# Sums of tiles 0 to 3 inside down's rounds, one sum of each pair in its bank, and down in a written order

## The chip, the cores and the metric

The kernel runs on one core of a Trainium2 chip. The core has five engines with a queue of instructions each: TensorE (PE, matrix products into PSUM banks), VectorE (DVE), ScalarE (ACT), GpSimd (POOL) and SyncE (SP), whose queue here only issues DMA transfers. An engine runs its queue in order, and an instruction that waits for another engine's result holds up everything behind it. The metric is the device time of one execution in microseconds, lower is better.

## The reference

An attention block with a learned feature map is multiplied by a gate from a SwiGLU block and added to the input. S = 2048 tokens, D = 1024, 32 heads of 32, F = 3584, all in fp32.

```python
xn = _layernorm(x)
q, k, v = split(xn @ wqkv)                      # 32 heads
phi_q = concat(softmax(q @ w_phi), softmax(-(q @ w_phi)))   # phi_k alike
kv, z = phi_k^T v, sum over s of phi_k
o = (phi_q @ kv) / (phi_q . z + 1e-6)
s = o @ wo
out = (silu(xn @ w1) * (xn @ w3)) @ w2
return x + s * silu(out)
```

## The kernel before

All large products run on PE as 128x128x512 matmuls in three passes over split operands (a high and a low part, written by `split`: ACT casts the high part, DVE subtracts it to get the low one). Each 2x2 block product is done with seven products instead of eight (`ORDER`: A11 x B11, A12 x B21, S2 x T2, S1 x T1, S3 x T3, S4 x B22, A22 x T4), whose partial sums share three kinds of PSUM bank: `a` for A12, `b` for A11, S2, S3 and A22 one after another, `c` for S1 and S4. A product can go into a bank only when the result of the one before has been read from it.

The stages are: gate and up products with w1 and w3; keys, values and queries; *down* (the product with w2); and the *output stage* (attention, product with wo, gate, store).

**The query stage** (`query_features`) does not divide the softmax of the queries. It writes exp(q - max) and exp(min - q) of every tile of 128 tokens to DRAM (`e_d`) and the ratio of the two sums to `rho_d`. The division by `phi_q . z` is left for later: for a tile t the *sums* are formed in steps. `z_products` multiplies e by z on POOL (two halves of 128x1024), `z_sums` reduces by head on DVE (two halves), `weigh` multiplies by rho on POOL, `add_pairs` adds pairs of partition groups with one small matmul on PE into a tile called `us`, `invert` takes the reciprocal on DVE, `factors` multiplies by rho again on POOL. Then `scale` multiplies e by the factors and `turn_e` transposes it, both in two halves on DVE.

**Down** runs in 56 rounds: round r = 8 kb + i, for 7 slices kb of w2's rows and 8 pairs i of token tiles. A round has seven products of six matmuls, in the order of `TURN`: S1, A11, S3, A12, S4, S2, A22, numbered m = 0 to 6. A11, A12 and S2 belong to the round's own pair (`old` is the pair before, whose S1, S3, S4 and A22 run one round late). `first_parts` and `second_parts` make the split operands from h, loaded by `load_h` into `hr`: `sm` (L953), then halves named `af` and `as` (L93), and `s` (L965, L966). The results are summed over kb in `acc`, two slabs of 128x1024 for a pair: DVE adds a bank to it (L1171), and in the first slice ACT copies it (L1165). The first block C11 gets two products: ACT copies A11's bank into `u` (L1168), POOL adds `u` (L1169), and DVE adds bank a. Weights of w2 come through `load_b` into a ring of 24 buffers, which later also takes wo's tiles (`load_wo`, `wos`) and small tables.

In the last slice (rounds 48 to 55) `gate` applies silu on ACT to the pair that was finished two rounds before and stores it to `g_d` from SP's queue, and the dictionary `pieces` puts the sums of tiles 0, 1 and 2 at given products: for tile 0 the products at (1,5), the sums at (2,5) and (2,6), add_pairs at (3,0), scale at (3,5) and (3,6), turn_e at (4,5) and (4,6); for tile 1 from (5,5) to (7,1); for tile 2 products and sums from (7,5) on. The first number is i, the second m.

**What sets the order.** `in_order` lists the engines whose instructions run in the order in which they are written; for others a scheduler sets the order at build time. In down it is SP's alone up to round 5, no engine's from round 6 to 47, and all engines' from round 48 on, output stage included. Waits between engines are put in by the framework in any case.

**The output stage** goes over 16 tiles t. For each, `out_half(t, 0)` and `out_half(t, 1)` multiply the attention of the tile (`oT`) by wo, 24 matmuls each; between them come `scale` and `turn_e` of tile t+1, the sums' steps for tiles t+2 and t+3, `gated` (DVE multiplies by the gate `g`, POOL adds x), and `attend(t+1, c)`, 64 small matmuls into `po`, from which ACT and DVE make the next `oT`.

Of the kernel before, what the change touches and what calls it, by code (L numbers as in the profile page):

```python
# [17 lines left out]
P = 128  # L18
# [11 lines left out]
def tile_kernel(ctx: ExitStack, tc: tile.TileContext, x, wkT, wqT, wv, wphi, wo, w1, w3, w2, out):  # L30
# [151 lines left out]
    small.tile([P, PAD], F, name="pad", bufs=1)  # L182
# [740 lines left out]
    def ring(name):  # L923
        nonlocal ring_at
        k = ring_at % 24
        ring_at += 1
        if k < 8:
            return bpa.tile([P, 2, 512], R, name=name, tag=f"ra{k}")
        if k < 20:
            return bpb.tile([P, 2, 512], R, name=name, tag=f"rb{k}")  # L930
        return late_rw[(k - 20) // 2][:, k % 2]
# [51 lines left out]
    ready = []  # L983
# [12 lines left out]
    for c in range(3):  # L996
# [5 lines left out]
        for pos, i in enumerate(order):  # L1002
            nxt, end = {}, pos + 1 == len(pairs)

            def steps():
                halves = []
                for j in range(7):
# [10 lines left out]
                    if end and j in NEXT[c]:  # L1018
                        wbn.update(fetch(3 + c, NEXT[c][j]))
                    if end and last and j in (1, 4):  # L1020
                        ready.append(a_first(0, 0) if j == 1 else a_second(*ready[0]))
# [23 lines left out]
    wos, xrs, ezs, us = {}, [], [], {}  # L1045
# [14 lines left out]

    def load_kvz():
        e0 = [slot_f("e0") for _ in range(2)]
        zb, kvs, w, own = (slot_f(name) for name in ("zb", "kvs", "rho", "own"))
        for a in range(2):
            for s in range(2):
                sl = slice(64 * a + 32 * s, 64 * a + 32 * s + 32)
                nc.sync.dma_start(zb[sl], z_d[s:s + 1].rearrange("s c g n -> s (c g n)").to_broadcast([32, D]))
                nc.sync.dma_start(kvs[sl].rearrange("p (j n) -> p j n", j=4),
                                  kv_d[:, :, s].rearrange("j f c g d -> f j (c g d)"))
            nc.gpsimd.memset(w[64 * a:64 * a + 32], 1.0)  # L1070
            nc.sync.dma_start(w[64 * a + 32:64 * a + 64].rearrange("p (t g n) -> p t g n", t=NT, g=2),
                              rho_d[a].rearrange("g i t n -> i t g n"))
        pairs_of = own[:, :P]
        nc.gpsimd.memset(pairs_of, 0.0)
        for n in range(4):
            sl = slice(32 * n, 32 * n + 32)
            for s in range(2):
                m = 32 * (n // 2 * 2 + s)
                nc.gpsimd.tensor_copy(pairs_of[sl, m:m + 32], ident[sl, sl])
        ezs.extend(slot_f("ez") for _ in range(2))  # L1080
        return (e0, zb, kvs.rearrange("p (j c g d) -> p j c g d", j=4, c=2, g=4),
                w.rearrange("p (t g c h) -> p t c g h", t=NT, g=2, c=2), own)
# [7 lines left out]
    def load_e(t):  # L1090
        if t >= NT:
            return
        for a in range(2):
            for s in range(2):
                sl = slice(64 * a + 32 * s, 64 * a + 32 * s + 32)
                src = e_d[t][64 * a:64 * a + 64, :, s * 512:s * 512 + 512].rearrange("(g i) c n -> i c g n", g=2)
                if t:
                    m = (12, 14, 8, 10)[t % 4]
                    nc.sync.dma_start(slabs[sl, m:m + 2].rearrange("i c (g n) -> i c g n", g=2), src)
                else:  # L1100
                    for c in range(2):
                        nc.sync.dma_start(e0[c][sl].rearrange("i (g n) -> i g n", g=2), src[:, c])

    def col(m):
        return own[:, P + 64 * m:P + 64 * m + 64]

    def wide(v):
        return v.rearrange("p (c g h) -> p c g h", c=2, g=2)

    def z_products(t):  # L1110
        if t < NT:
            for c in range(2):
                e = e_slab(t, c).rearrange("p (g n) -> p g n", g=2)
                nc.gpsimd.tensor_mul(ezs[c].rearrange("p (g n) -> p g n", g=2), e,  # L1114
                                     zb[:, c * 512:c * 512 + 512].unsqueeze(1).to_broadcast([P, 2, 512]))

    def z_sums(t, c):
        if t < NT:
            nc.vector.tensor_reduce(col(1 + t % 2)[:, 32 * c:32 * c + 32], ezs[c].rearrange("p (n f) -> p n f", f=DH),  # L1119
                                    axis=AX.X, op=OP.add)  # L1120

    def weigh(t):
        if t < NT:
            nc.gpsimd.tensor_mul(wide(col(0)), wide(col(1 + t % 2)), w_all[:, t])

    def add_pairs(t, tag):
        if t < NT:
            us[t] = ps.tile([P, 512], F, name="us", tag=tag, bufs=1)[:, :64]
            nc.tensor.matmul(us[t], own[:, :P], col(0), start=True, stop=True)

    def invert(t):
        if t < NT:
            nc.vector.reciprocal(col(3 + t % 2), us.pop(t))

    def factors(t):
        if t < NT:
            nc.gpsimd.tensor_mul(wide(col(0)), wide(col(3 + t % 2)), w_all[:, t])

    def scale(t, c):
        if t < NT:  # L1140
            e3 = e_slab(t, c).rearrange("p (n f) -> p n f", f=DH)
            nc.vector.tensor_mul(e3, e3, col(0)[:, 32 * c:32 * c + 32].unsqueeze(2).to_broadcast([P, H, DH]))

    def turn_e(t, c):
        if t < NT:
            nc.vector.transpose(et_slab(t, c), e_slab(t, c))  # L1146

    def product(kb, i, bank, r, ao, b, an, bn):
        c11, c12, c21, c22 = acc_of(i)
        first = b not in bank  # L1150
        if first:

            tag = "kv" if b == "c" and r > 1 and r % 3 == 2 else f"bk{b}"
            bank[b] = ps.tile([P, 512], F, name=f"bank{b}", tag=tag, bufs=1 if tag == "kv" else BANKS[b])
# [9 lines left out]
        if kb == 0 and an in ("A11", "S2", "S1", "A22"):  # L1164
            nc.scalar.copy(c, pb)  # L1165
        elif an == "A11":
            u = work.tile([P, 512], F, name="u", tag="h1", bufs=2)
            nc.scalar.copy(u, pb)  # L1168
            nc.gpsimd.tensor_add(c, c, u)  # L1169
        else:  # L1170
            nc.vector.tensor_add(c, pb, c)  # L1171
# [5 lines left out]
    pieces = {  # L1177
        (1, 5): [lambda: z_products(0)],
        (2, 5): [lambda: z_sums(0, 0)],
        (2, 6): [lambda: z_sums(0, 1), lambda: weigh(0)],  # L1180
        (3, 0): [lambda: add_pairs(0, "kv")],
        (3, 1): [lambda: invert(0), lambda: factors(0)],
        (3, 5): [lambda: scale(0, 0)],
        (3, 6): [lambda: scale(0, 1)],
        (4, 5): [lambda: turn_e(0, 0)],
        (4, 6): [lambda: turn_e(0, 1)],
        (5, 5): [lambda: z_products(1)],
        (6, 5): [lambda: z_sums(1, 0)],
        (6, 6): [lambda: z_sums(1, 1), lambda: weigh(1)],
        (7, 0): [lambda: add_pairs(1, "kv")],  # L1190
        (7, 1): [lambda: invert(1), lambda: factors(1)],
        (7, 5): [lambda: z_products(2)],
        (8, 4): [lambda: z_sums(2, 0)],
        (8, 6): [lambda: z_sums(2, 1)],
    }
    old, banks, first, second = None, {}, ready[0], None
    ahead = {}
# [63 lines left out]
    for k in range(14, 16):  # L1261
        load_wo(k)
# [125 lines left out]
```

## Time and profile before

| | us |
|---|---|
| median of 3 runs (2399.95 to 2402.06) | 2401.25 |
| the profiled execution's own time | 2401.13 |
| its span, first to last instruction | 2399.3 |
| PE busy | 2360.1 |
| down's first product begins | 1629.89 |
| A11 of round 50, of round 55 begins | 2103.01, 2162.99 |
| first `po` of the output stage | 2176.80 |

The profile is of one execution. Times in it are microseconds from the span's start. A row of a timeline has the start, the duration (of a merged row, from the first start to the last end), the engine, the line of the kernel, the operation with its output and inputs, the shape and the number of instructions; a bracket gives the idle time before it and the instruction that ended that. PE's ends are modelled, and neighbouring products overlap by a sixth of a microsecond in the rows, so PE's pace is read from start to start. "PEclk" or "granted clock" is the share of PE's clock that was granted.

### The profile page before, as it was taken

The numbers are of one execution on the slowest core, as the hardware profiler recorded it, in microseconds if no ns is written. First come the engines' busy times: TensorE is split into PE (matmuls) and PEld (weight loads), VectorE is DVE, ScalarE is ACT, GpSimd is POOL, SyncE is SP. The second block draws the span as 40 slices with busy tenths as digits, with TensorE's granted clock in tenths as the row PEclk, the third lists the DMA queues.
The fourth block names the chain that finished last, engine by engine and source line by source line (L and its number), as shares of the span: only waits on it lengthen the run. The fifth ranks groups of instructions, "written<-read, shape, count | busy, mean of one in ns | idle before, by whom it ended". The sixth has DMA issues, their size and how long they took to land. (4 is left out here: it accounts for less than half of the span.)

```text
span 2399.3 us, 37196 instructions
## 1 busy us (share of the span) xinstructions
PE 2360.1 (98%) x14354; PEld 1938.1 (81%) x14354; DVE 1776.9 (74%) x2779; ACT 855.1 (36%) x1501; POOL 253.2 (11%) x249
## 2 busy tenths in 40 slices
PE   7999999999999999999999999999999999998999
PEld 6788888888888888888788888887888888876887
DVE  8877787765788888864566666777687887796775
ACT  6445455443454555442222212334322222241000
POOL 1000000000000000000000001331011111223662
PEclk9999999999999999999999999999999999999999
DMA  5446799976988888865978878976543344448773
GB/s 213 149 157 207 238 349 336 327 254 201 288 298 295 294 271 304 278 233 189 372 265 303 288 234 336 374 263 238 184 176 109 129 176 176 136 151 299 220 206 120
DMA packets 290066, 578.00 MB, mean 241 GB/s; under 512 B 24529, under 2 KB 140385, under 8 KB 287201
## 3 DMA queue, kind: packets, MB, share of 16 engines
q1 hardware_dynamic: 285280, 558.85, 68.3%
q10 hardware_dynamic: 4608, 16.78, 1.7%
q8 instruction: 113, 1.85, 0.3%
q14 instruction: 65, 0.52, 0.1%
HBM read 370.54 MB, written 205.00 MB: 240 GB/s over the span
## 5 line engine op out<-in xcount | busy, mean ns | idle before, releaser
L93 DVE TENSOR_TENSOR bo<-rw,bo 128x512 fp32r<-128x512 f32 x336 | 230.8, 689 | 158.7 <-ACT bo L92 158.5
L92 ACT CAST bo<-rw 128x512 fp32r<-128x512 f32 x336 | 206.4, 617 | 12.9 <-DMA w_d2B<-w2o 3.3
L1159 PE MATMUL bankb<-bo,as 128*128 128x512 f32 x816 | 201.8, 390 | 3.3 <-DVE acc L1171 2.8
L1159 PEld LDWEIGHTS bankb<-bo,as 128*128 128x128 f32 x816 | 153.0, 188 | 36.4 <-DVE acc L1171 3.3
L598 PE MATMUL bankb<-op0S,bo 128*128 128x512 f32 x672 | 164.6, 394 | 1.9 <-ACT op0S L92 1.2
L598 PE MATMUL bankc<-op0S,bo 128*128 128x512 f32 x672 | 162.2, 391 | 0.0
L598 PE MATMUL bankb<-op1S,bo 128*128 128x512 f32 x672 | 161.4, 389 | 0.1
L598 PE MATMUL bankc<-op1S,bo 128*128 128x512 f32 x672 | 161.2, 389 | 0.0
L598 PE MATMUL bankb<-op0A,bo 128*128 128x512 f32 x672 | 159.6, 391 | 0.8 <-DVE bo L93 0.5
L598 PE MATMUL bankb<-op1A,bo 128*128 128x512 f32 x672 | 157.6, 390 | 0.0
L771 POOL MEMSET ev<- 128x32 f32 x32 | 4.2, 132 | 1428.0 <-DMA xoA<-xo_d0A 1072.7
L598 PEld LDWEIGHTS bankb<-op0S,bo 128*128 128x128 f32 x672 | 126.3, 189 | 29.0 <-ACT op0S L92 1.6
L598 PEld LDWEIGHTS bankb<-op1A,bo 128*128 128x128 f32 x672 | 125.9, 188 | 27.3 <-DVE u L641 1.3
L598 PEld LDWEIGHTS bankb<-op1S,bo 128*128 128x128 f32 x672 | 126.0, 188 | 26.6 <-ACT u L633 0.5
L1159 PE MATMUL bankc<-bo,as 128*128 128x512 f32 x576 | 147.3, 391 | 0.0
L598 PEld LDWEIGHTS bankc<-op1S,bo 128*128 128x128 f32 x672 | 126.1, 188 | 26.2
L598 PEld LDWEIGHTS bankb<-op0A,bo 128*128 128x128 f32 x672 | 125.2, 188 | 26.9 <-DVE bo L93 0.8
L598 PEld LDWEIGHTS bankc<-op0S,bo 128*128 128x128 f32 x672 | 125.4, 188 | 25.7
L1301 PE MATMUL pm<-wos,oT 128*128 128x512 f32 x576 | 136.9, 394 | 3.6 <-DVE oT L1292 1.8
L1301 PEld LDWEIGHTS pm<-wos,oT 128*128 128x128 f32 x576 | 106.5, 188 | 28.6 <-DMA wos<-wo_d 3.2
L1159 PEld LDWEIGHTS bankc<-bo,as 128*128 128x128 f32 x576 | 109.0, 189 | 22.8
L1171 DVE TENSOR_TENSOR acc<-bankb,acc 128x512 f32<-128x512 f32 x152 | 103.9, 685 | 21.1 <-PE bankb L1159 16.9
(252 smaller groups left out, 4428.6 us busy)
## 6 DMA issues: line engine op xcount, KB each, us to landing
rw<-in_w SPq DMA_DIRECT2D x112, 512.0 KB, 4.5
hr<-h_d SPq DMA_DIRECT2D x56, 512.0 KB, 3.6
h_d<-h SPq DMA_DIRECT2D x111, 256.0 KB, 4.8
xoS<-xo_d0S SPq DMA_DIRECT2D x44, 512.0 KB, 6.1
xoS<-xo_d1S SPq DMA_DIRECT2D x44, 512.0 KB, 5.8
xoA<-xo_d0A SPq DMA_DIRECT2D x33, 512.0 KB, 5.4
xoA<-xo_d1A SPq DMA_DIRECT2D x33, 512.0 KB, 4.3
e_d<-eq ACTq DMA_DIRECT2D x32, 512.0 KB, 6.1
```

The costliest lines, as they stand in the source:

```text
L92: nc.scalar.copy(hi, src)
L93: (by or nc.vector).tensor_sub(lo, src, hi.bitcast(F))
L598: nc.tensor.matmul(bank[b], bos[tb, f][bn][:, w, k], ao[an][:, u, k], start=first and n == 0, stop=LAST[b] == an and n == 11, skip_group_c ...
L771: nc.gpsimd.memset(v[:, :, DH:], 1.0)
L1159: nc.tensor.matmul(bank[b], t[:, u, pos + k], bos[kb, bn, k][:, w], start=first and n == 0, stop=LAST[b] == an and n == 5, skip_group_chec ...
L1171: nc.vector.tensor_add(c, pb, c)
L1301: nc.tensor.matmul(p, oTs[t, h][:, a, k], wos[c, 4 * h + k][:, b], start=n == 0, stop=n == 3 * ND - 1)
```

## The change

It has four parts.

1. The sums of tiles 0 to 3 move from the last slice and the output stage into rounds 18 to 44. Tile by tile and half by half, every three rounds, `load_part` loads half an e again into one buffer `er`, POOL multiplies it in place by z (12 products later), and DVE reduces it into a column of `early_z` (4 products later). After the eighth half, rho is loaded over `er`, and for all four tiles at once `weigh_early` (POOL), `add_early` (one matmul of 256 columns on PE), `invert_early` (two reciprocals of 128x128 on DVE) and `weigh_early` again make the factors, by round 44. Rounds 48 to 55 keep only scale and turn_e of tile 0, at (2,5), (2,6), (4,5), (4,6). The output stage forms sums for tiles 4 to 15 alone.
2. C11: at a round's start, from slice 1 on, ACT copies C11 from `acc` into a new bank a (`seed`), the product A12 adds to it there, ACT copies the bank back, and POOL adds `u`. DVE's add of bank a is gone in these rounds.
3. All engines of down follow the written order from round 0. In each round the second parts of the operands are formed between m = 0 and 2, the next round's first parts at m = 3 and 4; h is loaded two rounds ahead.
4. The ring has 22 buffers; the other two make room for z and `er`. The loads of wo and of the next slice's last weights are issued right after the product that frees their buffer.

Line numbers after the change: L1201 is ACT's copy into acc, L1209 DVE's add, L1184 the seed, L1204 the copy into u, L1206 the copy of bank a, L1207 POOL's add, L1112 the product with z, L1115 its reduction, L1172 scale, L1175 turn_e.

At the seam of query stage and down, ACT's queue before (L841 is the exponential of the query stage, L846 its store, L1165 the copy of a bank into acc, L92 a cast):

```order
L867 COPY q<-bankc 128x512
L92 CAST as<-s_14207 128x512
L92 CAST af<-hr 128x512
L841 ACTIVATE eq<-eq 128x1024
L92 CAST as_14287<-sm 128x256
L846 DMA e_d_236<-eq 128x1024
L92 CAST af<-hr 128x512
L92 CAST as<-hr 128x512
L1165 COPY acc<-bankb 128x512
L841 ACTIVATE eq<-eq 128x1024
```

and the same place after:

```order
L867 COPY q<-bankc 128x512
L92 CAST as<-s_14207 128x512
L841 ACTIVATE eq<-eq 128x1024
L846 DMA e_d_236<-eq 128x1024
L841 ACTIVATE eq<-eq 128x1024
L846 DMA e_d_232<-eq 128x1024
L1201 COPY acc<-bankb 128x512
L92 CAST af<-hr 128x512
```

The first copy of a down product and the casts of rounds 1 and 2 stood ahead of the second exponential and stand behind it now.

In the last slice, DVE's queue before, from the end of round 50 into round 51 (L1119 is z_sums, L1133 invert, the names with numbers are split operands):

```order
L93 TENSOR_TENSOR as_18127<-sm,as_18127 128x256
L1171 TENSOR_TENSOR acc<-bankb,acc 128x512
L1119 TENSOR_REDUCE own<-ez 128x32
L1171 TENSOR_TENSOR acc<-bankb,acc 128x512
L1119 TENSOR_REDUCE own<-ez 128x32
L1171 TENSOR_TENSOR acc<-bankc,acc 128x512
L93 TENSOR_TENSOR as<-hr,as 128x512
L965 TENSOR_TENSOR s_18185<-hr,sm 128x256
L966 TENSOR_TENSOR s_18185<-hr,sm 128x256
L1133 RECIPROCAL own<-us 128x64
L1171 TENSOR_TENSOR acc<-bankb,acc 128x512
```

and the same place after:

```order
L93 TENSOR_TENSOR as_18225<-sm,as_18225 128x256
L1209 TENSOR_TENSOR acc<-bankb,acc 128x512
L1172 TENSOR_TENSOR e_18010<-e_18010,early_z 128x1024
L1209 TENSOR_TENSOR acc<-bankb,acc 128x512
L1172 TENSOR_TENSOR e_18011<-e_18011,early_z 128x1024
L1209 TENSOR_TENSOR acc<-bankc,acc 128x512
L93 TENSOR_TENSOR as<-hr,as 128x512
L963 TENSOR_TENSOR s_18281<-hr,sm 128x256
L964 TENSOR_TENSOR s_18281<-hr,sm 128x256
L1209 TENSOR_TENSOR acc<-bankb,acc 128x512
```

Reduction and reciprocal are gone from these rounds, and scale has moved up by a round into their slots.

In the output stage, DVE's queue before, for the first tile (L1292 makes an oT, L1142 is scale, L1146 turn_e, L1309 the product with g):

```order
L1292 TENSOR_TENSOR oT<-po,oT 128x2x4x64 x2
L1142 TENSOR_TENSOR acc<-acc,own 128x1024 x2
L1146 STREAM_TRANSPOSE acc<-acc 128x1024 x2
L1309 TENSOR_TENSOR g<-pm,g 128x512
L1133 RECIPROCAL own<-us 128x64
L1292 TENSOR_TENSOR oT<-po,oT 128x2x4x64
L1119 TENSOR_REDUCE own<-ez 128x32
L1292 TENSOR_TENSOR oT<-po,oT 128x2x4x64
```

and after (L1326 makes an oT, L1343 is the product with g):

```order
L1326 TENSOR_TENSOR oT<-po,oT 128x2x4x64 x2
L1172 TENSOR_TENSOR acc<-acc,early_z 128x1024 x2
L1175 STREAM_TRANSPOSE acc<-acc 128x1024 x2
L1343 TENSOR_TENSOR g<-pm,g 128x512
L1326 TENSOR_TENSOR oT<-po,oT 128x2x4x64 x2
```

The reciprocal and the reductions behind the product with g are gone.

The core of the diff:

```diff
     def ring(name):
         nonlocal ring_at
-        k = ring_at % 24
+        k = ring_at % 22
...
+    def load_part(n):
+        for a, s, sl in strips():
+            nc.sync.dma_start(halves(er[sl]), e_part(n // 2, a, s)[:, n % 2])
+
+    def weighted(dst, e, c):
+        nc.gpsimd.tensor_mul(halves(dst), halves(e), zb[:, c * 512:c * 512 + 512].unsqueeze(1).to_broadcast([P, 2, 512]))
+
+    def summed(dst, e, c):
+        nc.vector.tensor_reduce(of_half(dst, c), by_head(e), axis=AX.X, op=OP.add)
+
+    def weigh_early():
+        nc.gpsimd.tensor_mul(early_z, early_z, w_all[:, :256])
+
+    def add_early():
+        us["early"] = ps.tile([P, 512], F, name="us", tag="kv", bufs=1)
+        nc.tensor.matmul(us["early"][:, :256], consts, early_z, start=True, stop=True)
+
+    def invert_early(k):
+        u = us.pop("early") if k else us["early"]
+        nc.vector.reciprocal(early_z[:, k * P:k * P + P], u[:, k * P:k * P + P])
...
+    def seed(i, bank, r):
+
+        bank["a"] = new_bank("a", r)
+        nc.scalar.copy(bank["a"], acc_of(i)[0])
...
-        elif an == "A11":
-            u = work.tile([P, 512], F, name="u", tag="h1", bufs=2)
-            nc.scalar.copy(u, pb)
-            nc.gpsimd.tensor_add(c, c, u)
+        elif kb and an == "A11":
+            bank["u"] = work.tile([P, 512], F, name="u", tag="h1", bufs=2)
+            nc.scalar.copy(bank["u"], pb)
+        elif kb and an == "A12":
+            nc.scalar.copy(c, pb)
+            nc.gpsimd.tensor_add(c, c, bank["u"])
         else:
             nc.vector.tensor_add(c, pb, c)
...
+    for n in range(2 * EARLY):
+        at_ = 7 * 18 + 21 * n
+        piece(at_, lambda n=n: load_part(n))
+        piece(at_ + 12, lambda n=n: weighted(er, er, n % 2))
+        piece(at_ + 16, lambda n=n: summed(early(n // 2), er, n % 2))
+    piece(at_ + 17, load_weights)
+    piece(at_ + 30, weigh_early)
+    piece(at_ + 33, add_early)
+    piece(at_ + 35, lambda: invert_early(0))
+    piece(at_ + 37, lambda: invert_early(1))
+    piece(at_ + 39, weigh_early)
...
+    for k, do in enumerate((scale, scale, turn_e, turn_e)):
+        piece(7 * (50 + k // 2 * 2) + 5 + k % 2, lambda k=k, do=do: do(0, k % 2))
+    in_order(ENG.SP, ENG.PE, ENG.Activation, ENG.DVE, ENG.Pool)
     for r, new in enumerate(steps):
...
-        if r == 0:
-            in_order(ENG.SP)
-        elif r == 6:
-            in_order()
-        elif end and i == 0:
-            in_order(ENG.SP, ENG.PE, ENG.Activation, ENG.DVE, ENG.Pool)
...
+        if r + 2 < len(steps) - 1:
+            ahead[r + 2] = load_h(*steps[r + 2])
...
+        if r and new:
+            gen2 = second_parts(*parts)
+        if r + 1 < len(steps) - 1:
+            gen1 = first_parts(ahead.pop(r + 1))
+        if kb and new:
+            seed(i, bank, r)
...
+            if m < 3 and r and new:
+                then = next(gen2)
+            if m in (3, 4) and r + 1 < len(steps) - 1:
+                first = next(gen1)
...
+            if i + 1 == len(pairs) and an in FIRST:
+                n = BNAMES.index(bn)
+                for k in range(2):
+                    if end:
+                        load_wo(2 * n + k)
+                    elif k:
+                        load_b(kb + 1, 4 + n)
+            for do in pieces.pop(7 * r + m, ()):
+                do()
...
-        weigh(t + 2)
+        if t + 2 >= EARLY:
+            weigh(t + 2)
...
-        z_products(t + 3)
+        if t + 3 >= EARLY:
+            z_products(t + 3)
...
-        add_pairs(t + 2, "us")
-        invert(t + 2)
-        factors(t + 2)
+        if t + 2 >= EARLY:
+            add_pairs(t + 2)
+            invert(t + 2)
+            factors(t + 2)
```

More of the change, by code (lines that the diff above doesn't have):

```diff
@@ L1019, in steps @@
                         wbn.update(fetch(3 + c, NEXT[c][j]))
+                    if end and last and j == 5:
+                        ahead[1] = load_h(0, 1)
                     if end and last and j in (1, 4):
@@ L1058, in slot_f, with strips @@
         return flat(ring(name).bitcast(F))
-    def load_kvz():
-        e0 = [slot_f("e0") for _ in range(2)]
-        zb, kvs, w, own = (slot_f(name) for name in ("zb", "kvs", "rho", "own"))
+    def strips():
         for a in range(2):
             for s in range(2):
[L1066 to L1082, printed above, removed]
@@ L1122, in weigh @@
[L1122 to L1137, printed above, removed]
+        for a, s, sl in strips():
+            if t:
+                m = (12, 14, 8, 10)[t % 4]
+                nc.sync.dma_start(slabs[sl, m:m + 2].rearrange("i c (g n) -> i c g n", g=2), e_part(t, a, s))
+            else:
+                for c in range(2):
+                    nc.sync.dma_start(halves(e0[c][sl]), e_part(0, a, s)[:, c])
```

203 lines of the change are left out of this document (99 added, 104 removed).

## The prediction, made before the changed kernel ran

> **What bounds the kernel now.** I read the page's first part, then whom TensorE (PE) waits for from the start of down on, then PE's instructions in order of time, and last the other engines beside the places where PE stands still. First the page's busy times, then the top of the list of PE's waits in 1630 to 2399 us (total, number of times, longest):
>
> ```profile
> PE 2360.1 (98%) x14354; PEld 1938.1 (81%) x14354; DVE 1776.9 (74%) x2779; ACT 855.1 (36%) x1501; POOL 253.2 (11%) x249
> ```
>
> ```profile
> PE us L1129 <- POOL own L1124: 4.7, 4, 2.3
> PE bankb L1159 <- DVE acc L1171: 3.2, 2, 2.8
> ```
>
> PE is the bound, and the change adds almost no work to it and takes almost none away. So the time can fall only by what PE loses to waiting inside the stages that change, and rise only by new waits. PE's timeline in down shows where it loses (start, duration, and the wait in brackets; "bankb<-bo,af" is A11, the second product of a round; the row at 2103.01 holds its first two matmuls of six):
>
> ```profile
> 1646.03 1.52 PE L1159 MATMUL bankb<-bo,af 128*128 128x512 f32 x6
> ...
> 2103.01 0.61 PE L1159 MATMUL bankb<-bo,af 128*128 128x512 f32 x2
> ...
> 2116.41 0.43 PE L1129 MATMUL us<-own 128*128 128x64 f32 x2 [2.26 <-POOL own L1124]
> 2116.65 2.18 PE L1159 MATMUL bankb<-bo,af 128*128 128x512 f32 x6
> ...
> 2127.90 1.52 PE L1159 MATMUL bankb<-bo,af 128*128 128x512 f32 x6
> ...
> 2137.42 1.52 PE L1159 MATMUL bankb<-bo,af 128*128 128x512 f32 x6
> 2138.78 1.52 PE L1159 MATMUL bankb<-late,as 128*128 128x512 f32 x6
> ...
> 2147.22 2.09 PE L1159 MATMUL bankb<-bo,as 128*128 128x512 f32 x6 [2.84 <-DVE acc L1171]
> 2149.11 2.72 PE L1159 MATMUL bankc<-bo,as 128*128 128x512 f32 x6
> ...
> 2162.75 0.43 PE L1129 MATMUL us<-own 128*128 128x64 f32 x2 [1.38 <-POOL own L1124]
> 2162.99 1.64 PE L1159 MATMUL bankb<-bo,af 128*128 128x512 f32 x6
> ```
>
> A round takes 2137.42 - 2127.90 = 9.52 us, so 1.36 a product. From A11 of round 2 (1646.03) to that of round 50 (2103.01) are 48 rounds in 456.98 us, 9.52 each: the middle of down loses nothing, and nothing can be won there. From round 50 to round 55 (2162.99) are five rounds in 59.98 us instead of 47.60: 12.4 us are lost. The three brackets explain 6.5 of them; most of the rest are matmuls that run slowly after a wait (2.09 and 2.72 us for products that take 1.52 by the same count elsewhere).
>
> **The change, part by part.**
>
> *The sums leave the last rounds.* The 2.26 and 1.38 us are PE waiting for the chain reduce, weigh, add_pairs, which is gone from rounds 48 to 55. The 2.84 us is VectorE (DVE) being late, and its reason stands beside it on GpSimd (POOL); first DVE, then POOL:
>
> ```profile
> 2135.72 0.68 DVE L1171 TENSOR_TENSOR acc<-bankb,acc 128x512 f32<-128x512 f32 x1
> ...
> 2139.78 1.76 DVE L93 TENSOR_TENSOR as<-hr,as 128x512 fp32r<-128x512 f32 x1
> 2141.46 2.61 DVE L965 TENSOR_TENSOR s<-hr,sm 128x256 f32<-128x256 f32 x1
> 2144.00 2.56 DVE L966 TENSOR_TENSOR s<-hr,sm 128x256 f32<-128x256 f32 x1
> ...
> 2147.30 0.69 DVE L93 TENSOR_TENSOR as<-s,as 128x512 fp32r<-128x512 f32 x1
> ...
> 2153.07 0.42 DVE L965 TENSOR_TENSOR s<-hr,sm 128x256 f32<-128x256 f32 x1
> ...
> 2159.30 1.21 DVE L1119 TENSOR_REDUCE own<-ez 128x32 f32<-128x1024 f32 x1
> ```
>
> ```profile
> 2140.95 5.33 POOL L1114 TENSOR_TENSOR ez<-acc,zb 128x1024 f32<-128x1024 f32 x2
> ```
>
> While POOL multiplies the two halves of tile 1 (2.66 us each), two subtractions of SBUF tiles, 0.42 us a few rows on, take 2.61 and 2.56. After the change no such product runs in the last eight rounds. The scale and turn_e of tile 0 stay there, in slots that DVE can afford, since the add of bank a into C11 (one L1171, 0.68 us) leaves DVE in every round. I take all 12.4 us as won. The lower end: one wait like the 2.84 is left, with the slow matmuls behind it, 2.84 + (2.09 - 1.52) + (2.72 - 1.52) = 4.6, so 7.8.
>
> *The sums in rounds 18 to 44.* Eight times POOL multiplies one half, 2.66 us, behind its own add of the round, and DVE reduces it a round later (1.21 us). Behind the blocked DVE instruction stands the add of product S2, and PE needs that add before S3 of the next round goes into the same bank. Before, the S2 add ends at 2135.72 + 0.68 = 2136.40 and S3 starts at 2138.78: 2.4 us of room, and about 3.0 with the C11 add gone. One blocked instruction costs 2.61 - 0.42 = 2.2 us. So nothing on PE; the cover left is 0.8 us, and the rivals price what comes without it. The added loads on SP's queue land long before their use: a part of e is issued 12 products (16 us) ahead of its product, rho 16 products ahead of add_early, against this row (KB each, us to landing):
>
> ```profile
> acc<-e_d SPq DMA_DIRECT2D x60, 256.0 KB, 6.2
> ```
>
> *One add_early for two add_pairs in down.* The matmul of 64 columns holds PE for 2116.65 - 2116.41 = 0.24 us; 256 columns four times that, 1.0 us lost (0.5 to 1.3). The old two are inside the 12.4.
>
> *The bank sum.* Per round ScalarE (ACT) gets two more copies of 128x512, 0.58 us each by the row below, POOL and PE nothing. The seed waits only for results eight rounds old. The copy of bank a stands ahead of the next round's casts in ACT's queue: A12 ends 4 products, 5.4 us, into the round, copy, casts and DVE's halves take under 3 us, and A11 of the next round comes at 10.9. Hidden, with over 2 us left.
>
> *Down in a written order from its first round.* Nothing to win in the middle, as shown. The seam with the query stage changes: the copy of A11's bank now stands behind both exponentials in ACT's queue. ACT, POOL, DVE and PE there:
>
> ```profile
> 1630.03 1.06 ACT L841 ACTIVATE eq<-eq 128x1024 f32<-128x1024 f32 x1 [3.87 <-POOL eq L840]
> ...
> 1632.54 0.58 ACT L1165 COPY acc<-bankb 128x512 f32<-128x512 f32 x1
> 1635.25 1.06 ACT L841 ACTIVATE eq<-eq 128x1024 f32<-128x1024 f32 x1 [2.14 <-POOL eq L840]
> ```
>
> ```profile
> 1628.77 1.23 POOL L840 TENSOR_TENSOR eq<-mm,q 128x512 f32<-128x512 f32 x1
> 1633.16 1.05 POOL L839 TENSOR_TENSOR eq<-q,mm 128x512 f32<-128x512 f32 x1 [3.16 <-ACT acc L1165]
> ```
>
> ```profile
> 1637.48 0.68 DVE L840 TENSOR_TENSOR eq<-mm,bankb 128x512 f32<-128x512 f32 x1
> ```
>
> ```profile
> 1633.17 1.67 PE L1159 MATMUL bankb<-bo,as 128*128 128x512 f32 x6 [0.40 <-ACT acc L1165]
> ...
> 1636.06 1.52 PE L1159 MATMUL bankb<-bo,af 128*128 128x512 f32 x6
> ```
>
> In the new order DVE forms the last tile's maxima early, so POOL goes on at 1630.0 and ends some 2.2 us later; the second exponential ends at 1633.3, its store is issued, and the copy ends at about 1634.3 instead of 1633.1. That delays S2 by 1.1 us. DVE's half of "af" for round 1 now comes behind the query's last L840, which two moved reductions bring forward to about 1636.3; add, subtraction and half (0.68 + 0.42 + 0.69) end at 1638.0, where PE wants it at 1637.5: 0.5 more. Before lost 0.45 between 1636.06 and 1646.03 (9.97 for a round), which then has no cause. Net 1.1 us lost (0 to 3).
>
> *The output stage.* No sums for tiles 2 and 3 in its first two tiles, and the loads of wo begin inside the last round. PE, DVE, SP's queue:
>
> ```profile
> 2198.95 5.28 PE L1301 MATMUL pm<-wos,oT 128*128 128x512 f32 x22 [1.60 <-DVE oT L1292]
> 2204.53 0.43 PE L1129 MATMUL us<-own 128*128 128x64 f32 x2 [0.30 <-POOL own L1124]
> 2205.31 0.85 PE L1286 MATMUL po<-acc,kvs 64*32 64x64 f32 x64 [0.35 <-DVE acc L1146]
> ...
> 2219.11 0.43 PE L1129 MATMUL us<-own 128*128 128x64 f32 x2 [0.79 <-POOL own L1124]
> 2219.90 0.85 PE L1286 MATMUL po<-acc,kvs 64*32 64x64 f32 x64 [0.35 <-DVE acc L1146]
> ```
>
> ```profile
> 2197.20 0.69 DVE L1309 TENSOR_TENSOR g<-pm,g 128x512 f32<-128x512 f32 x1 [12.36 <-DMA g<-g_d]
> 2197.80 0.55 DVE L1133 RECIPROCAL own<-us 128x64 f32<-128x64 f32 x1
> ```
>
> ```profile
> 2168.17 4.97 SPq L1049 DMA_DIRECT2D wos<-wo_d  x8
> ```
>
> The start is held by transfers: PE resumes at 2198.95 behind DVE, which waited for g until 2197.20. Of this 0.5 us go with the reciprocal. The first wo loads wait for A11 and A12 of the last round (from 2162.99 on) and one gate's store, so they leave about 1.7 us before 2168.17; between 0 and 1.7 us come back, I take 1.0. At the next tile 0.30 + 0.24 + 0.35 = 0.9 go, at the one after 0.79 + 0.35 = 1.1; us of tile 4 stays there. Sum 3.5 us (0.5 to 5.5).
>
> *Sum:* 12.4 - 1.0 - 1.1 + 3.5 = 13.8 us less. The profiled execution took 2401.13 us (span 2399.3), so 2387.3; the median of the runs is 2401.25, 0.1 more: 2387.4.
>
> *A rule against this size.* PE's granted clock (0.92, the third number from the end) falls in the stretch after the 2.84 us wait:
>
> ```profile
> 2150.00:2160.00 10.00, 10.00 (x42) 8.19 (x41) 8.83 (x17) 5.29 (x9) 1.30 (x1) 0.92 0.68 188
> ```
>
> The Trainium skill, page "TensorE: Matmul & The Clock Gate", section "What's actually happening", says that the clock halves after at least one idle window of about 3.4 us. By that rule none of these waits, 2.84 us at most, would slow a matmul, and only the 6.5 us in brackets would come back: 13.8 - 12.4 + 6.5 = 7.9 us, 2393.4. The trace disagrees (0.92), so I keep the 12.4, which is measured as a whole.
>
> **The rivals.**
>
> *Half the gain.* A wait like that of 2147 stays, since scale, turn_e and POOL's add still meet on DVE in the last rounds (-4.6), and the output stage stays with its transfers (0.5 in place of 3.5): 13.8 - 4.6 - 3.0 = 6.2, 2395. For it: the 12.36 us wait for g. Against: the 2.61 and 2.56 us stood beside a product that is gone.
>
> *Slower: the eight products block DVE.* If each half product holds up two SBUF instructions instead of one, and POOL's add of the same round a third (1.76 - 0.69 = 1.1), then 2 x 2.2 + 1.1 - 3.0 = 2.5 us of waiting per product, and with the slow matmuls behind it (12.4 lost for 6.5 waited, 1.9 times) 8 x 2.5 x 1.9 = 38 us: 2425. It decides from 13.8 / (8 x 1.9) = 0.9 us per product on. For it: two instructions in a row were held up at 2141.46 and 2144.00. Against: there POOL ran two products in a row, here one. The Trainium skill, page "SBUF — State Buffer", section "SBUF: two separate sides", says that of DVE and GpSimd the loser of their shared port blocks for the winner's whole instruction. The 2.61 us agree, for one instruction per product.
>
> *No change: the written order costs what the waits cost.* 13.8 us over 48 rounds are 0.29 us a round, in ACT's queue ahead of the casts. Against: the round from 2127.90 to 2137.42 ran in the same written order, with two activations on ACT besides, and took the plain 9.52.
>
> **How the numbers follow.** Less than 0.2% (4.8 us) can't be told from no change. Likeliest case 0.55, 2382 to 2391.5: seam at 0 and output at 5.5 below, a left-over wait above. Half the gain 0.20, 2391.5 to 2396.4. No change 0.09: 0.6 to 1.2 us per product, or the third rival. Slower 0.16. So faster 0.75, same 0.09, slower 0.16; 2382 to 2400 holds the first two and half of the third, about 8 in 10.
>
> **What would show it.** Right: A11 of rounds 18 to 55 9.52 us apart, with one exception of about 1 us at add_early; no wait of PE over 1 us for DVE or POOL in down; DVE subtractions of 2.6 us in every third round from 19 on; some 1.5 us of waits for ACT and DVE at the seam; us of tile 4 without a wait. Wrong: PE waiting for "acc" of DVE after each half product, or for wo and g as long as before.

## The result and the profile after

The changed kernel takes 2410.34 us (median of 6 runs, 2408.6 to 2411.39), the kernel before 2400.95 beside it (2399.95 to 2402.06). The ratio is 1.0038, 95% interval 1.0025 to 1.0051: slower by 9.4 us, where 2387.4 was forecast. The profiled execution of the changed kernel took 2408.6 us, its span is 2406.8.

By stage, from PE's timelines of both profiled executions (the third column is experiment e1, below):

| us | before | after | e1 |
|---|---|---|---|
| first product of down begins | 1629.89 | 1639.07 | 1631.71 |
| down, to the first `po` | 546.91 | 544.05 | 535.71 |
| output stage, from the first `po` to the start of the last `pm` | 217.87 | 218.94 | 217.98 |
| span | 2399.3 | 2406.8 | 2390.1 |

9.2 us are already lost when down begins, and 8.6 of them at the end of gate and up (1143.62 after 1135.02), a stage in which no instruction of any engine has changed or moved. Down itself became only 2.9 us shorter. So I looked for waits, first in the page's busy times, then in the list of PE's waits for 1639 to 2183 us, which is the whole of down after the change and has one row:

```profile
PE 2371.8 (99%) x14348; PEld 1934.4 (80%) x14348; DVE 1763.1 (73%) x2729; ACT 909.5 (38%) x1597; POOL 257.2 (11%) x243
```

```profile
PE bankb L1195 <- ACT acc L1201: 1.2, 1, 1.2
```

The waits went as forecast: of the 2.26, 2.84 and 1.38 us nothing is left, and the 1.2 us are the seam. But PE is busy 11.7 us longer with as much work. A table of stretches, for PE alone (busy time and matmuls, then granted clock, DMA share and GB/s), shows it. Before:

```profile
800.00:900.00 100.00, 100.00 (x442) 1.00 0.83 280
1900.00:2000.00 100.00, 100.00 (x443) 1.00 0.36 129
```

and after:

```profile
800.00:900.00 100.00, 100.00 (x437) 1.00 0.86 293
1900.00:2000.00 100.00, 100.00 (x435) 1.00 0.47 158
```

PE never stands still in these stretches, its granted clock is 1.00, and yet it gets through 437 and 435 matmuls instead of 442 and 443. The products have become longer one by one. PE's timeline in gate and up (L598 is the product there, "op1A" and "op1S" are operand tiles, read from start to start), before:

```profile
674.46 5.60 PE L598 MATMUL bankb<-op1A,bo 128*128 128x512 f32 x24
679.90 2.88 PE L598 MATMUL banka<-op1A,bo 128*128 128x512 f32 x12
682.62 2.88 PE L598 MATMUL bankb<-op1S,bo 128*128 128x512 f32 x12
685.34 2.88 PE L598 MATMUL bankc<-op1S,bo 128*128 128x512 f32 x12
```

and the same products after:

```profile
679.35 5.67 PE L598 MATMUL bankb<-op1A,bo 128*128 128x512 f32 x24
684.86 2.96 PE L598 MATMUL banka<-op1A,bo 128*128 128x512 f32 x12
687.66 2.90 PE L598 MATMUL bankb<-op1S,bo 128*128 128x512 f32 x12
690.39 2.88 PE L598 MATMUL bankc<-op1S,bo 128*128 128x512 f32 x12
```

Before, every product of twelve takes 2.72 us, 227 ns a matmul. After, the one from op1A into bank a takes 687.66 - 684.86 = 2.80, 233 ns, while those from op1S take 2.72 or 2.73. It depends on the operand tile. In down it makes the rounds (A11 to A11) 9.57 to 9.73 us long instead of 9.52, without a wait, but for those at the seam and the one with add_early. From round 50 to round 51 it is 9.73:

```profile
2120.46 1.54 PE L1195 MATMUL bankb<-bo,af 128*128 128x512 f32 x6
...
2130.19 1.54 PE L1195 MATMUL bankb<-bo,af 128*128 128x512 f32 x6
```

What can differ between op1A and op1S is where they lie. One line of the change says where everything lies, and neither the part on the change above nor the prediction speaks of it:

```diff
-    small.tile([P, PAD], F, name="pad", bufs=1)
+    early_z = small.tile([P, 256], F, name="early_z", bufs=1)
```

PAD is 32 floats, so 128 bytes of each partition became 1024. The tile lies near the left end of SBUF, and the pools behind it on that side (work, q, the operand slots, part of the ring) all start 896 bytes later. The pools on the right side (the other part of the ring, two operand slots, `late`) stay. I took each matmul's two addresses from the built programs, the moving tile's (the 512 columns) and the weights' (128x128), and the time from its start to the next from the traces (those of 200 to 260 ns with another 128x512 matmul behind them, which leaves out waits):

```
distance of moving tile and weights, modulo 256 bytes
            0                      128
before      9539 of 227.0 ns       none
after       6957 of 227.5 ns       2614 of 232.7 ns
```

Over 226.7 ns, the undisturbed pace, these gaps add up to 2.8 us before and to 5.7 + 15.7 = 21.4 us after: 18.6 us more, of which 5.1 in gate and up, 2.8 in keys, values and queries, 8.3 in down and 2.5 in the output stage. The rest of the 8.6 us lost by the end of gate and up are waits of PE there, 6.2 us after 2.8, above all for DVE's `bo` (3.2 after 0.5); the last section returns to them. Whether the distance is the cause, the experiments had to show.

### The profile page after: what moved, and what is told of

Same layout as the page of the kernel before. It is cut to its first block, busy times and chain, and to the rows that moved or that the text cites. A ratio compares the mean times of both kernels' runs of the same rounds, so it can differ in the third digit from the quotient of the medians.

```text
span 2406.8 us, 37213 instructions
## 1 busy us (share of the span) xinstructions
PE 2371.8 (99%) x14348; PEld 1934.4 (80%) x14348; DVE 1763.1 (73%) x2729; ACT 909.5 (38%) x1597; POOL 257.2 (11%) x243
## 4 chain that ended last, share of the span: by engine, by line
PE 91%; DMA 3%; DVE 3%; SPq 1%; ACT 1%; issue 1%; POOL 0%; DVEq 0%; ACTq 0%; POOLq 0%
PE bankb L598 24%; PE bankb L1195 13%; PE bankc L598 12%; PE bankb L794 7%; PE pm L1335 6%; PE bankc L1195 6%; PE banka L598 6%; PE bankc L794 3%; PE banka L1195 3%; PE bankb L861 3%; PE banka L794 2%; PE bankc L861 1%; PE pkv L779 1%; PE po L1320 1%; DMA g_d<-acc 1%; PE pw L247 1%
## 5 line engine op out<-in xcount | busy, mean ns | idle before, releaser
L1195 PE MATMUL bankb<-bo,as 128*128 128x512 f32 x960 | 238.3, 392 | 1.2 <-ACT acc L1201 1.2
L1195 PEld LDWEIGHTS bankb<-bo,as 128*128 128x128 f32 x960 | 180.1, 188 | 42.2 <-ACT acc L1201 1.6
L92 ACT CAST bo<-rw 128x512 fp32r<-128x512 f32 x336 | 206.4, 617 | 14.0 <-DVE w2o L93 4.4
L1335 PE MATMUL pm<-wos,oT 128*128 128x512 f32 x672 | 168.6, 399 | 4.5 <-DMA wos<-wo_d 2.7
L598 PE MATMUL bankb<-op0S,bo 128*128 128x512 f32 x672 | 164.7, 394 | 1.9 <-ACT op0S L92 1.2
L598 PE MATMUL bankb<-op1S,bo 128*128 128x512 f32 x672 | 161.8, 390 | 0.7 <-ACT u L633 0.7
L598 PE MATMUL bankc<-op0S,bo 128*128 128x512 f32 x672 | 162.4, 391 | 0.0
L598 PE MATMUL bankc<-op1S,bo 128*128 128x512 f32 x672 | 161.6, 389 | 0.5 <-DVE bo L93 0.5
L598 PE MATMUL bankb<-op1A,bo 128*128 128x512 f32 x672 | 159.9, 392 | 2.2 <-DVE bo L93 2.2
L598 PE MATMUL bankb<-op0A,bo 128*128 128x512 f32 x672 | 159.8, 392 | 0.8 <-DVE bo L93 0.5
L1195 PE MATMUL bankc<-bo,as 128*128 128x512 f32 x624 | 160.4, 392 | 0.0
L1335 PEld LDWEIGHTS pm<-wos,oT 128*128 128x128 f32 x672 | 123.1, 188 | 36.9 <-DMA wos<-wo_d 5.7
L598 PEld LDWEIGHTS bankb<-op1A,bo 128*128 128x128 f32 x672 | 125.8, 188 | 31.2 <-DVE bo L93 2.6
L598 PEld LDWEIGHTS bankb<-op0S,bo 128*128 128x128 f32 x672 | 126.3, 190 | 29.1 <-ACT op0S L92 1.6
L598 PEld LDWEIGHTS bankb<-op1S,bo 128*128 128x128 f32 x672 | 126.1, 188 | 28.1 <-ACT u L633 1.1
L598 PEld LDWEIGHTS bankc<-op1S,bo 128*128 128x128 f32 x672 | 126.1, 188 | 27.1 <-DVE bo L93 0.9
L598 PEld LDWEIGHTS bankb<-op0A,bo 128*128 128x128 f32 x672 | 125.2, 188 | 27.0 <-DVE bo L93 0.8
L598 PEld LDWEIGHTS bankc<-op0S,bo 128*128 128x128 f32 x672 | 125.4, 188 | 25.8
L1195 PEld LDWEIGHTS bankc<-bo,as 128*128 128x128 f32 x624 | 117.1, 188 | 26.3
L1209 DVE TENSOR_TENSOR acc<-bankb,acc 128x512 f32<-128x512 f32 x152 | 102.4, 684 | 36.2 <-PE bankb L1195 34.6
```

Source lines behind the costliest of these rows:

```text
L92: nc.scalar.copy(hi, src)
L598: nc.tensor.matmul(bank[b], bos[tb, f][bn][:, w, k], ao[an][:, u, k], start=first and n == 0, stop=LAST[b] == an and n == 11, skip_group_c ...
L1195: nc.tensor.matmul(bank[b], t[:, u, pos + k], bos[kb, bn, k][:, w], start=first and n == 0, stop=LAST[b] == an and n == 5, skip_group_chec ...
L1335: nc.tensor.matmul(p, oTs[t, h][:, a, k], wos[c, 4 * h + k][:, b], start=n == 0, stop=n == 3 * ND - 1)
```

## Experiments

The theory: a matmul takes longer when its moving tile and its weights don't lie a multiple of some power of two apart, and the change lost by this what it won. The rival: the changed work slows PE (more reads and writes of banks by ACT, a fuller DVE, more loads), and the addresses go along with it by chance.

**e1: the change with the left side moved by 1024 bytes instead of 896.**

```diff
     early_z = small.tile([P, 256], F, name="early_z", bufs=1)
+    small.tile([P, PAD], F, name="pad", bufs=1)
```

> The changed kernel with 32 more floats beside early_z, so that every tile on the left side of SBUF lies 1024 bytes further than in the kernel before, in place of 896. No instruction differs. Theory (addresses: a product whose moving tile and weight tile stand 128 bytes apart modulo 512 takes 229 to 237 ns a matmul instead of 227): all 128x512 matmuls back at 227 ns, the 18.7 us of longer matmuls and some 3.5 us of waits behind them gone, 2388 us (2384 to 2393), first A11 of down near 1636 us. Rival (the changed work itself slows PE, by ACT's added reads and writes of banks or a fuller DVE): 2410 us as before, since the work is the same.

Measured: 2391.47 us (2389.45 to 2392.31, 5 runs), 0.9962 of the kernel before (0.995 to 0.9975). That is 18.9 us less than the change as it was, from 32 floats that nothing reads. Down begins at 1631.71 in the profiled execution, earlier than the 1636 expected. PE's matmuls per 100 us, and A11 of rounds 53 and 54:

```profile
800.00:900.00 100.00, 100.00 (x442) 1.00 0.83 278
1800.00:1900.00 100.00, 100.00 (x443) 1.00 0.52 175
```

```profile
2134.68 1.52 PE L1196 MATMUL bankb<-bo,af 128*128 128x512 f32 x6
...
2144.20 1.52 PE L1196 MATMUL bankb<-bo,af 128*128 128x512 f32 x6
```

The pace is that of before, and a round takes 9.52 us in the last slice too. The rival is out: the changed work is all there.

**e2, e3, e4: the kernel before, with nothing but its pad changed.**

```diff
-PAD = 32
+PAD = 256      # e2, left side moved by 896 bytes
+PAD = 288      # e3, by 1024
+PAD = 96       # e4, by 256
```

> The kernel before with its pad of 32 floats made 256 floats, so that the left side of SBUF moves by the same 896 bytes as in the change, and nothing else. Theory (addresses): slower by 18 to 24 us, 2419 to 2425 us, with matmuls of 229 to 238 ns wherever the moving tile is on the right side. Rival (the changed work): 2401 us.

> The kernel before with the pad made 288 floats: the left side moves by 1024 bytes, two times 512. Theory (only the distance of the two operands modulo 512 bytes counts): 2401 us, matmuls of 227 ns. Rival (any move of the left side costs, or it is the absolute address that counts): slower by 5 us or more.

> The kernel before with the pad made 96 floats: the left side moves by 256 bytes, so operands from the two sides stand 256 bytes apart modulo 512. Open by the theory, which has seen only the distances 0 and 128: if the period is 256 bytes, 2401 us; if it is 512, slower by an amount between 5 and 25 us.

Measured, against 2400.19 us of the kernel before beside them: e2 2418.7 (1.0077, 1.0064 to 1.009; just under the 2419 to 2425 expected), e3 2401.11 (1.0006, 0.9997 to 1.0015), e4 2400.56 (1.0, 0.9991 to 1.0009). The pad alone costs the kernel before 18.5 us, what the gaps of the changed kernel had added up to (18.6), and PE's stretches in e2 look like those after the change:

```profile
800.00:900.00 100.00, 100.00 (x438) 1.00 0.83 284
1900.00:2000.00 100.00, 100.00 (x436) 1.00 0.38 132
```

A move by 1024 or by 256 bytes costs nothing that can be measured, so the period is 256 bytes or less.

**e5: the distance by itself.** PE runs series of 64 matmuls, with nothing beside them:

```diff
+    for k in range(64):
+        nc.tensor.matmul(bank, weight[:, w:w + 128], move[:, m:m + 512], start=k == 0, stop=k == 63)
```

> A kernel that computes nothing of the reference: after a warm-up, sixteen series of 64 matmuls 128x512 in fp32r, each into a bank of its own whose name tells the distance in bytes from weight tile to moving tile (thirtytwo, sixtyfour, ninetysix, half = 128, onesixty, oneninetytwo, twotwentyfour, full = 256, one_and_half = 384, two = 512, minus_half = -128); both_moved has both tiles 128 bytes further, pair_by_pair changes from one matmul to the next between neither and both moved, weights_alone moves the weights of every second one. No other engine works and no transfer runs beside them. Theory (addresses alone): 227 ns at 0, 256, 512 and both_moved, 229 to 237 at 128, 384 and -128; open between them. If the distance to the next weights counts, pair_by_pair is slow. Rival (it takes the traffic of other engines on those tiles): 227 ns in every series.

PE's timeline; the first column is the start, so a series of 64 lasts until the next row's start:

```profile
71.06 14.67 PE L49 MATMUL gap_zero<-move,weight 128*128 128x512 f32 x64
85.56 15.10 PE L49 MATMUL gap_thirtytwo<-move,weight 128*128 128x512 f32 x64
100.50 14.82 PE L49 MATMUL gap_sixtyfour<-move,weight 128*128 128x512 f32 x64
115.16 15.09 PE L49 MATMUL gap_ninetysix<-move,weight 128*128 128x512 f32 x64
130.09 15.09 PE L49 MATMUL gap_half<-move,weight 128*128 128x512 f32 x64
145.02 15.15 PE L49 MATMUL gap_onesixty<-move,weight 128*128 128x512 f32 x64
160.01 15.10 PE L49 MATMUL gap_oneninetytwo<-move,weight 128*128 128x512 f32 x64
174.95 15.09 PE L49 MATMUL gap_twotwentyfour<-move,weight 128*128 128x512 f32 x64
189.88 14.69 PE L49 MATMUL gap_full<-move,weight 128*128 128x512 f32 x64
204.41 15.09 PE L49 MATMUL gap_one_and_half<-move,weight 128*128 128x512 f32 x64
219.34 14.69 PE L49 MATMUL gap_two<-move,weight 128*128 128x512 f32 x64
233.86 15.04 PE L49 MATMUL gap_minus_half<-move,weight 128*128 128x512 f32 x64
248.74 14.73 PE L49 MATMUL both_moved<-move,weight 128*128 128x512 f32 x64
263.31 14.79 PE L49 MATMUL pair_by_pair<-move,weight 128*128 128x512 f32 x64
277.93 15.03 PE L49 MATMUL weights_alone<-move,weight 128*128 128x512 f32 x64
292.79 14.69 PE L49 MATMUL again_zero<-move,weight 128*128 128x512 f32 x64
```

At 0, 256 and 512 bytes 64 matmuls take 14.50 to 14.53 us, 227 ns each. At 32, 96, 128, 160, 192, 224, 384 and -128 they take 14.88 to 14.99, 232 to 234 ns, at 64 it is 14.66, 229 ns. Both tiles moved by 128 bytes: 14.57. So it is the distance alone, it takes no other engine and no transfer, and the rival's 227 ns everywhere is wrong. The series pair_by_pair (14.62, 228.5 ns) has every matmul at distance 0 from its own weights and at 128 from the next ones; in weights_alone (14.86) every second matmul stands at 128 from its own weights, the others at 128 from the next ones. By these two series the time seems to depend on both; with one execution of each, that and the share of each stay open.

The Trainium skill, page "SBUF — State Buffer", section "Who interferes with whom", gives PE two independent read ports, one for the moving operand and one for the loads of weights, and says that PE never waits on anyone. In e5 PE waits for no other engine, and yet the distance of its own two operands makes 233 ns out of 227, which two independent ports would not lead one to expect. Where in the chip the two meet, no run here shows.

**e8: the distance mended from the other side.** The left side stays where the change put it, and the right side moves by 128 bytes:

```diff
-    edge[1].tile([P, 120], F, name="edge_r")
+    edge[1].tile([P, 152], F, name="edge_r")
```

> The changed kernel as it is, with the strip at the right end of SBUF 128 bytes wider (120 floats made 152), so that every tile on the right side moves 128 bytes towards the left one, and the distances between the two sides are multiples of 256 again, while the left side stays where the change put it. If the distance of the two operands counts: as e1, 2388 to 2393 us, matmuls of 227 ns. If the address of one operand counts, on the left or on the right: 2400 us or more, with longer matmuls still there.

Measured: 2392.97 us (2391.53 to 2399.18, 9 runs), 0.9975 of before (0.9965 to 0.9984). All matmuls are at 227 ns again (9541, mean 227.0). The profiled execution is the slowest of the nine: PE waits 2.6 us once for DVE's `bo` in gate and up, and down, which then takes 535.7 us, begins at 1636.95. It is the distance, not the address of either side.

**e7: what the bank sum is worth,** on top of e1:

```diff
-        if kb and new:
-            seed(i, bank, r)
...
-        elif kb and an == "A11":
-            bank["u"] = work.tile([P, 512], F, name="u", tag="h1", bufs=2)
-            nc.scalar.copy(bank["u"], pb)
-        elif kb and an == "A12":
-            nc.scalar.copy(c, pb)
-            nc.gpsimd.tensor_add(c, c, bank["u"])
+        elif an == "A11":
+            u = work.tile([P, 512], F, name="u", tag="h1", bufs=2)
+            nc.scalar.copy(u, pb)
+            nc.gpsimd.tensor_add(c, c, u)
```

> e1 with A11 and A12 added apart as in the kernel before (ACT copies A11 and POOL adds it, DVE adds A12 from its bank; no seed, no copy of bank a), the rest as changed. If the bank sum is what gives DVE the room for the sums in rounds 18 to 44: rounds with a half product take up to 0.5 us longer, 2391 to 2396 us. If the 2.4 us of room that DVE had before are enough: 2391.5 us, rounds of 9.52 us. If the seed and the copies on ACT cost PE something that the trace does not show as a wait: less than 2391.

Measured: 2389.72 us (2387.73 to 2390.53), 0.995 of before (0.9937 to 0.9962), and down takes 535.71 us, as in e1. Its rounds take 9.52 us, the second case expected. The median is 1.8 us below that case's 2391.5, but down begins at 1629.50 in the profiled execution, 2.2 us earlier than in e1, and the intervals of e1 and e7 overlap, so neither a gain nor a loss by the bank sum is shown. It is hidden, as forecast, and the sums don't need it: DVE's room before was enough.

**e6 and e9: why the output stage won nothing.** In e1 PE waits there for (from 2155 us on):

```profile
PE pm L1336 <- DMA wos<-wo_d: 3.0, 8, 0.7
PE po L1321 <- DVE acc L1176: 1.8, 1, 1.8
PE pm L1336 <- DVE oT L1327: 1.5, 2, 1.2
```

DVE is late because it has waited 12.78 us for g:

```profile
2187.80 0.69 DVE L1344 TENSOR_TENSOR g<-pm,g 128x512 f32<-128x512 f32 x1 [12.78 <-DMA g<-g_d]
```

e6 issues the loads of g for tiles 0 and 1 earlier (on top of e1):

```diff
+        if new is None:
+            load_g(0)
...
-    load_g(0)
...
+        if t == 0:
+            load_g(1)
         if t + 4 < NT:
             load_e(t + 4)
...
-        load_g(t + 1)
+        if t:
+            load_g(t + 1)
```

> e1 with the loads of g for tile 0 issued before the last eight loads of wo, and those for tile 1 before the load of e for tile 4. Theory (the start of the output stage is held by the place of the g loads in SP's queue): DVE's waits of 12.78 and 5.89 us for g shrink, with them PE's waits of 1.19, 0.35 and 1.75 us there: 1.5 to 3.3 us less than e1, 2388 to 2390 us. Rival (the transfers themselves are full, so any order costs the same): 2391 us, with longer waits for wos in place of those for oT.

Measured: 2388.69 us (2385.83 to 2390.09), 0.9946 of before (0.9932 to 0.9959). DVE's wait for g is gone, and PE's waits in the output stage are now:

```profile
2172.98 0.69 DVE L1346 TENSOR_TENSOR g<-pm,g 128x512 f32<-128x512 f32 x1 [2.39 <-PE pm L1338]
```

```profile
PE pm L1338 <- DMA wos<-wo_d: 5.0, 10, 1.6
PE po L1323 <- DVE acc L1176: 0.6, 1, 0.6
PE us L1145 <- POOL own L1140: 0.3, 1, 0.3
```

6.3 us of waits became 5.9: what DVE no longer waits for, PE waits for at wos, and the output stage takes 217.60 us after 217.98. The median lies in the theory's range, but the stage goes by the rival: the 2.8 us between the medians of e6 and e1 are not the stage's, and the two intervals overlap. Down begins between 1627.28 (e6) and 1631.71 (e1) in the profiled executions of before, e1, e3, e4, e6, e7 and e9, which have the same work and the same pace up to there, but for the order at the seam. e9 then leaves out half of the loads (on top of e6):

```diff
     def load_wo(k):
+        if k > 7:
+            wos[1, k - 8] = wos[0, k - 8]
+            return
         t = ring("wos")
```

> e6 without the last eight of the sixteen loads of wo: the second half of each output row is computed with the first half's weights, so this part of the computation is not the reference's, and 4 MB less are moved around the start of the output stage. If the transfers hold that start (theory): PE's 5.0 us of waits for wos fall under 1.5, the output stage goes from 217.6 us to 212.5 to 214.5, the whole to some 2385 us. If it is DVE's chain of scale, turn_e and oT: 217 us, with waits for acc and oT in their place.

Measured: 2381.6 us (2381.41 to 2385.01), 0.9926 of before (0.9912 to 0.9939); the output stage takes 212.48 us, 5.1 less than in e6. PE's list there has one row, of 1.6 us, where under 1.5 was expected:

```profile
PE pm L1341 <- DMA wos<-wo_d: 1.6, 2, 1.4
```

So the transfers hold the start of the output stage by their amount; the other order, that of e6, won nothing. In e1 the 16 DMA engines are full there (the last three numbers are granted clock, DMA share and GB/s):

```profile
2170.00:2180.00 10.00, 8.77 (x95) 5.83 (x93) 5.02 (x5) 2.24 (x3) 0.00 (x0) 1.00 1.03 417
2180.00:2190.00 10.00, 7.00 (x86) 4.22 (x86) 2.20 (x4) 0.58 (x1) 0.81 (x1) 1.00 0.98 400
```

## Why the prediction was wrong

**The step that failed** is the first one: "So the time can fall only by what PE loses to waiting inside the stages that change, and rise only by new waits." It took a product's 1.36 us at full granted clock for a constant. It depends on where the two operands lie, and the change moved one side of SBUF against the other. That is worth 18.6 us (by the gaps), 18.5 (e2 against before) or 18.9 us (the change against e1), more than the whole forecast gain of 13.8, and none of the rivals had it: they all were waits. The 0.16 for "slower" was for PE waiting behind DVE, of which the trace has nothing, so the direction does not speak for that rival. That the three figures agree to 0.4 us is in part luck: executions of one kernel differ by 2 to 4 us, and the profiled ones are 15.9 (e2 and before) and 16.7 us (the change and e1) apart. Of the 2410.3 - 2387.4 = 22.9 us of error, this leaves 4.3, about what e1 shows: 2391.5 - 2387.4 = 4.1. The other steps can be judged on e1, where the pace is undisturbed.

- *The sums leave the last rounds, 12.4 us:* right, as a whole. Rounds 50 to 55 take 9.52 us each in e1. By the rule of the Trainium skill that the prediction weighed (page "TensorE: Matmul & The Clock Gate", section "What's actually happening") only 6.5 would have come back. The runs disagree with it: with waits of 2.84 us and less, the slow matmuls behind them went too. In before, PE's granted clock (third number from the end) is halved behind the waits of 2.26 and 2.84 us, and 1.00 behind the one of 1.38:

```profile
2117.60:2120.90 3.30, 3.30 (x9) 0.50 0.00 0
2148.30:2151.60 3.30, 3.30 (x9) 0.50 0.14 57
```

In e1 it is 1.00 over all of these rounds:

```profile
2100.00:2165.00 65.00, 65.00 (x288) 1.00 0.61 193
```

- *The sums in rounds 18 to 44, nothing on PE:* right, by another instruction than forecast. POOL's half product and DVE beside it in e1:

```profile
1816.78 2.85 POOL L1113 TENSOR_TENSOR room<-room 128x1024 f32<-128x1024 f32 x1
```

```profile
1817.90 2.01 DVE L93 TENSOR_TENSOR as<-sm,as 128x256 fp32r<-128x256 f32 x1
...
1824.33 1.21 DVE L1116 TENSOR_REDUCE early_z<-room 128x32 f32<-128x1024 f32 x1
...
1827.75 0.41 DVE L93 TENSOR_TENSOR as<-sm,as 128x256 fp32r<-128x256 f32 x1
```

A half of a split (0.41 us a round later) is held for 1.6 us and ends 0.28 us after the product, in place of a subtraction of 2.6 us. All eight products show this one instruction held, and PE does not notice. The rival of 2.5 us per product is out, and so is the written order at 0.29 us a round.
- *add_early, 1.0 us:* 0.48 in e1, where the round with it takes 10.00 us (A11 at 2039.01 and 2049.01) instead of 9.52. The estimate by columns was twice too large: the next product begins 0.24 us after the matmul of 256 columns, as it did after one of 64, and takes 0.22 us longer.
- *The seam, 1.1 us:* 0.8. A11 of rounds 0 to 2 come 6.94 and 10.03 us apart in e1, 6.17 and 9.97 before; the wait for ACT's copy is the 1.2 us above. The 0.45 us that I expected back in the second of these gaps did not come.
- *The bank sum, hidden:* right (e7).
- *The output stage, 3.5 us (0.5 to 5.5):* wrong, -0.1 us in e1. The term added up waits of PE for POOL and DVE one by one. They went, and what came next was not followed. The first loads of wo do leave earlier, 10.1 us before the first `po` in e1 instead of 8.6, as forecast, but the DMA engines are full behind them (above), and the load of g leaves no earlier, 10.4 us after the first `po` instead of 10.2. So g is used 20.38 us after it, 20.40 before. SP's queue in before and then in e1:

```profile
2187.01 0.32 SPq L1272 DMA_DIRECT2D g<-g_d  x1
```

```profile
2157.33 1.19 SPq L1051 DMA_DIRECT2D wos<-wo_d  x2
...
2177.82 0.32 SPq L1307 DMA_DIRECT2D g<-g_d  x1
```

And turn_e of tile 3, on a DVE that has just waited 5.89 us for the next g, costs PE the 1.8 us above (0.6 in e6, where that wait for g is gone). The rival "half the gain" had this part right (the output stage stays with its transfers), with 0.5 us.

By e1 the sum is 11.2 us won in down (10.3 forecast) and 0.1 lost in the output stage (3.5 won forecast). That is 2.7 us short of the forecast. The profiled execution of e1 (2391.91) is 4.6 us above the 2387.3 forecast for a profiled one, and the rest of that is the 1.8 us by which down begins later in it than in before's, inside the spread of 1627 to 1632 given above.

## What to carry to other kernels

Check the distance of moving tile and weights before any other explanation when a change alters a tile's size: of the distances tried here only the multiples of 256 bytes run at the full pace, and a tile of another size anywhere ahead of them on one side of SBUF changes it for all products that take one operand from each side. The sign in a profile is a busy PE at full granted clock that gets through fewer matmuls per 100 us, from a stage on that the change does not touch. And a wait that goes from the start of a stage whose transfers are full is won only if the transfers shrink too.

## What the runs showed of the hardware that I had not expected

A 128x512 matmul in fp32r (the type of the split operands) takes 227 ns when its moving tile lies 0, 256 or 512 bytes (modulo 256: 0) from its weights, 229 ns at 64 bytes, and 232 to 234 ns at 32, 96, 128, 160, 192, 224, 384 and -128 (e5). Nothing else has to run for it. In this kernel 2614 of its 9571 undisturbed 128x512 matmuls were at 128 bytes, and that was 0.8% of the time.

Executions of kernels with the same instructions and the same pace differ by some us in gate and up. In the profiled executions PE's longest wait for DVE's `bo` in 580 to 700 us is 2.2 us after the change, 2.6 in e8, 1.8 in e7, 1.4 in e4, 0.5 in e1, and none shows in before, so it goes neither with the distances nor with the change. Its cause was not looked for.
